# Two gate pieces in every step of part 1, and those of a split's step moved between its scores and its transposes

## The chip, the cores and the metric

The kernel runs on one core of one Trainium2 chip. A time is device microseconds (us) of one execution of the whole program. The engines are TensorE (PE; its weight loads are listed apart as PEld), VectorE (DVE), ScalarE (ACT), GpSimd (POOL) and SyncE (SP), which here only issues DMAs. Each works through its own queue of instructions in order, and they wait for each other by semaphores.

## The reference

A gated linear attention with a state per head, and a feed-forward block that multiplies two projections:

```python
# q, k, v, alpha: batch 4, heads 8, 768 positions, head size 48
for t in range(S):
    state = alpha[:, :, t, :, None] * state + einsum('bhd,bhe->bhde', k[:, :, t], v[:, :, t])
    y[:, :, t] = einsum('bhd,bhde->bhe', q[:, :, t], state)
x = y as (3072 tokens, 384)
out = ((x @ w1) * (x @ w2) @ w3) @ w_out      # d_ff 1024
```

The weights arrive as 64-bit floats.

## The kernel before

**Chunks and steps.** The 3072 positions are cut into 24 chunks of 128 (six per batch entry), and part 1 is a loop of 25 steps `n`, one chunk each. On TensorE a step holds, in this order: the state products of chunk n-1 (`attend_state`, L473 or L483), the scores of chunk n (`scores`, L431 with the lower halves of chunk n-1's attention, L420), the transposes of decayed q and k of chunk n+1 (`transposed`, L383, copied out of PSUM by ScalarE at L385), the attention of chunk n-1 (`attend`, L496; ScalarE copies y out at L493 and L498), the outer products of k and v of chunk n (`outer`, L395, taken over by VectorE at L405; none for the last chunk of a batch entry), and the sums of logarithms for chunk n+3 (`decays`, L348). VectorE masks the scores (L441, four instructions per step) and multiplies q and k by the decays (`decayed`, L361). ScalarE takes the logarithms of alpha (L326), rounds them (L330; VectorE makes the rest, L331) and makes the exponentials (L351, L352) out of the sums.

**Groups, splits, pieces.** Part 1 has room on TensorE for the first products of the feed-forward block. `EARLY` names five groups of finished chunks: four of three chunks (384 tokens) and one of four. A group begins with its split (`split_early`): x is cut into a rounded part (ScalarE, L536) and two rests (VectorE, L537 and L539), in one buffer for all groups, so a split has to wait until the products of the group before it are done. Then its gates follow: a gate is one tile of 128 of the 1024 columns, and makes x @ w1 and x @ w2 for it. Each of these two is one piece: nine matmuls of 384 columns (L569), six into one PSUM bank, which ScalarE empties (L578), and three into another, which VectorE adds (L580). After the second piece VectorE multiplies both (L617), and the product of the gate before is stored by a DMA (`store_ab`, L643, on SP's queue). The gates are generators that yield between their pieces; they lie in the queue `fill`, and `run(k)` issues the next k pieces. A group of four gates thus has eight pieces. The last group has sixteen, of which eight are left to part 2.

**Where the order comes from.** Group 0 is split in step 6, groups 1 to 4 in steps 9, 13, 17 and 21 (the steps with `n - 2 in begin`). Behind the transposes of that step the split is issued, and its gates are put into `fill`. `pieces` says how many a step issues: `run(pieces > 0)` behind the outer products, `run(pieces > 1)` behind the logarithms, `run(pieces > 2)` at the end of the step. In step 7 another `run(2)` stands behind the transposes. The framework turns this program into one queue per engine, chooses the eight PSUM banks, and may change the order of neighbours on ScalarE and VectorE; `after_marks` keeps instructions behind a named one on the same engine. Besides, `convert` works off the conversion of w1 and w2 from 64 bits a step at a time (L246 to L267, on ScalarE and VectorE).

**Part 2** makes the remaining gates, folds w3 and w_out together and makes the output. The change doesn't touch it.

Of the kernel before, what the change touches and what calls it, by code (L numbers as in the profile page):

```python
# [48 lines left out]
def kernel(  # L49
# [18 lines left out]
    N = B * NCH  # L68
# [37 lines left out]
    def bank():  # L106
        return ps.tile([C, 512], FP32, tag="bank", name="bank")
# [3 lines left out]
    def after_marks(*names):  # L111
        stack = ExitStack()
        for x in names:
            stack.enter_context(tc.issue_after(mark[x]))
        return stack
# [22 lines left out]
    def load_a(n):  # L138
        if paired(n):
            if n % 2 == 0:  # L140
                b, c = divmod(n, NCH)
                x = pairs[n // 2 % 2]
                nc.sync.dma_start(out=x.rearrange("p h s d -> p h (s d)"), in_=alpha[b, :, ds(c * C, 2 * C), :].rearrange("h (p s) d -> p h (s d)", s=2))
                st["a", n] = st["a", n + 1] = x
        elif n < N:
            st["a", n] = inp.tile([C, H, D], FP32, tag="ac", name="ac", bufs=2)
            nc.sync.dma_start(out=st["a", n], in_=rows(alpha, n))

    def load_kq(n):
        if n >= N:  # L150
            return
        st["kq", n] = inp.tile([C, 2, H, D], FP32, tag="kq", name="kq")
        nc.sync.dma_start(out=st["kq", n][:, 0], in_=rows(k, n))
        nc.sync.dma_start(out=st["kq", n][:, 1], in_=rows(q, n))

    def load_v(n):
        if n < N:
            st["v", n] = vs[n % len(vs)]
            (nc.gpsimd if 2 < n < 8 else nc.sync).dma_start(out=st["v", n][:, :, 0:D], in_=rows(v, n))
# [122 lines left out]
    def fetch(ahead=3):  # L282
        while weights and len(begun) < ahead:
            begun.append(weights.popleft())
            next(begun[-1])
# [17 lines left out]
    def store():  # L303

        while later:
            dst, src = later.popleft()
            nc.sync.dma_start(out=dst, in_=src)
# [64 lines left out]
    def transposed(n):  # L372
        if n >= N:
            return
        qk = qks[n % 3]
        qkT = work.tile([C, 2, NP, C], FP32, tag="qkT", name="qkT")

        tp = [bank().rearrange("p (i j c) -> p i j c", i=2, j=NP) for _ in range(2)]
        for i in range(2):
            for j in range(NP):  # L380
                for half in range(2):
                    s = ds(DP * half, DP)
                    nc.tensor.transpose(tp[half][:, i, j, :], qk[s, i, 2 * j:2 * j + 2, :], ident[s, s])  # L383
        for half in range(2):
            mark["qkT", n] = nc.scalar.copy(qkT[:, :, :, ds(DP * half, DP)], tp[half]).ins  # L385
        st["qkT", n] = qkT
# [30 lines left out]
    def attend_low(n, j, i):  # L417

        s, w = ds(DP * i, DP), (vts[n % 2][:, j, :] if i else st["v", n][:, 2 * j, :])
        nc.tensor.matmul(st["y", n][1][ds(DP * (1 - i), DP), j, :], w[s], st["ms", n][s, i, j, 0:DP],  # L420
                         start=(n % NCH == 0 and j == 0), stop=(j == NP - 1), skip_group_check=True)
# [94 lines left out]
    def load_early(e):  # L516

        first, chunks = EARLY[e]
        if chunks == 3:
            pieces = ((xb[0][:, XB - KM * TG:].bitcast(FP32), 3),)  # L520
        else:
            pieces = ((inp.tile([C, 2, H, D], FP32, tag="kq", name="kq").rearrange("p i h d -> p (i h d)"), 2),
                      *((inp.tile([C, H, D], FP32, tag="ac", name="ac", bufs=2).rearrange("p h d -> p (h d)"), 1) for _ in range(2)))
        st["xT", e], at = [], 0
        for x, width in pieces:
            x = x.rearrange("p (k t) -> p k t", k=KM)
            nc.sync.dma_start(out=x, in_=x_of(first + at, width))
            st["xT", e].append((x, ds(at * C, width * C)))
            at += width
# [174 lines left out]
    fill = deque()  # L704

    def run(pieces):

        for _ in range(pieces):
            if not fill:
                return  # L710
            try:
                next(fill[0])
            except StopIteration:
                fill.popleft()
# [22 lines left out]
    FIRST = 6  # L737
    begin = {FIRST - 3 + 4 * g: (g, range(FH if g < 4 else KF)) for g in range(5)}
    loads = {8: 1, 11: 2, 15: 3, 20: 4}

    def early_pair(n):
        return n in ends and n < FIRST

    for n in range(N + 1):
        if n >= FIRST:
            load_v(n + 2)
        if not 1 < n < FIRST:
            store()
        if n in loads:
            load_early(loads[n])  # L750
        if n != 1 and not 2 < n <= FIRST:
            load_a(n + 5)
        raws = (3, 3, 3, 3, 2, 2, 3, 3)[n] if n < 8 else 4
        for m in (n + 3,) * (n <= FIRST) + (n + 4,) * (n >= FIRST):
            load_kq(m)
            if 2 < n <= FIRST and m == n + 3:
                load_a(n + 5)
            if 1 < n < FIRST:
                store()
            if n < FIRST - 2:  # L760
                fetch(raws)
        late_state = early_pair(n - 1)
        if n and not late_state:
            attend_state(n - 1)
        if n < N:
            scores(n)
            if late_state:
                attend_state(n - 1)
        else:
            for j in range(NP):  # L770
                for i in range(2):
                    attend_low(n - 1, j, i)
        transposed(n + 1)
        if n == 1:
            decays(3)
            load_a(6)
            with after_marks(("e", 3)):
                logs(4)
        if n == FIRST + 1:
            run(2)  # L780
        if n - 2 in begin and n > FIRST:
            g, tiles = begin[n - 2]
            with after_marks(("ms", n), ("qkT", n + 1)):
                split_early(g)
            fill.extend(gate(g, f) for f in tiles)
        if n == FIRST:
            with after_marks("l", ("qkT", n + 1)):
                split_early(0)
            fill.extend(gate(0, f) for f in begin[n - 3][1])
        pieces = ((3, 3, 2, 0) if n > FIRST + 3 else (0, 3, 3, 0))[(n - FIRST) % 4] if n >= FIRST else 0  # L790
        if n == 0:
            with after_marks(("qkT", 0)):
                logs(2)
            decays(2)
            with after_marks(("e", 2)):
                logs(3)
        early, ready = n < FIRST, len(thirds) if n > 2 else n // 2
        marks = (*[("qkT", n + 1)] * (n < N - 1), *[("qk", n + 1), ("ms", n)] * early, *["x3"] * (n - 2 in begin and n > FIRST))
        if n < N - 2 and n != FIRST:
            with after_marks(*marks):  # L800
                convert(2 if early else 1, raws)
        with after_marks(*[("vt", n)] * turned(n)):
            advance(n)
        if n < FIRST:
            with after_marks("pool"):
                load_v(n + 2)
        if n:
            attend(n - 1)
        outer(n)
        if n > FIRST:  # L810
            third(ready)
        run(pieces > 0)
        if early:
            with after_marks(*marks):
                convert(1, raws)
        with after_marks(*[("ms", n)] * (n <= FIRST)):
            decayed(n + 2)
        if not early:
            with after_marks(*[("qkT", n + 1)] * (n < N - 4), *["scale"] * (n > FIRST)):
                logs(n + 4)  # L820
        if n == 4:
            load_early(0)
        convert(early and n > 0, raws)
        run(pieces > 1)
        if n:
            decays(n + 3)
        if n <= FIRST:
            third(ready)
        if 0 < n < FIRST:
            with after_marks(("e", n + 3)):  # L830
                logs(n + 4)
        if n == FIRST:
            with after_marks("x3", ("e", n + 3)):
                convert(2, raws)
        elif n < N - 2:
            convert(n == FIRST - 1 if early else n % 3 == 0, raws)
        if n == FIRST - 1:
            assert len(done) == 2 * KM
        turn_v(n + 1)
        run(pieces > 2)  # L840
        if n == N - 3:
            while begun:
                convert(1)
            weights.extend(load_out(j) for j in range(KF))
            fetch(4)
# [92 lines left out]
```

## Time and profile before

| | us |
|---|---|
| three runs | 456.66, 458.87, 460.57 (median 458.87) |
| the profiled execution | 456.97 |
| its span, first to last instruction | 455.2 |
| TensorE busy (4304 matmuls) | 442.2, 97% |
| its weight loads busy (4304) | 392.9, 86% |
| VectorE busy | 369.8, 81% |
| ScalarE busy | 279.3, 61% |
| GpSimd busy | 85.5, 19% |

The granted TensorE clock of the profiled execution is 0.999. A row of the profile names the kernel's line, the engine, the operation, the tile written and the tiles read, the shape, how often, the busy time and the mean in ns of one, and then the idle time just before with what ended it. Matmuls are pipelined and overlap in such rows, so lengths are better read from one start to the next. L569 is the line of a helper that issues all large matmuls; in part 1 it stands for the gates' pieces.

The steps of the stretch in question, by the start of their first matmul on TensorE (us from the span's start):

| step | 7 | 8 | 9 | 10 | 11 | 12 | 13 | 14 | 15 | 16 | 17 | 18 | 19 | 20 | 21 | 22 | 23 |
|---|---|---|---|---|---|---|---|---|---|---|---|---|---|---|---|---|---|
| start | 51.92 | 64.05 | 72.87 | 76.69 | 87.08 | 95.12 | 102.06 | 105.42 | 114.75 | 123.25 | 130.19 | 133.56 | 143.00 | 151.49 | 158.45 | 161.72 | 172.24 |
| length | 12.13 | 8.82 | 3.82 | 10.39 | 8.04 | 6.94 | 3.36 | 9.33 | 8.50 | 6.94 | 3.37 | 9.44 | 8.49 | 6.96 | 3.27 | 10.52 | 8.54 |
| pieces | 5 | 3 | 0 | 3 | 3 | 2 | 0 | 3 | 3 | 2 | 0 | 3 | 3 | 2 | 0 | 3 | 3 |

Steps 7, 13 and 19 have no state products, steps 11, 17 and 23 no outer products, steps 21 and later no logarithms.

### The profile page before, as it was taken

Reading aid. Unit: us, or ns where it says so; the run is one execution under the profiler, and the core shown is the slowest. Engines: PE = TensorE matmul, PEld = TensorE weight load, DVE = VectorE, ACT = ScalarE, POOL = GpSimd, SP = SyncE. Lnnn points to the kernel's source line nnn. Section 1 sums busy time; section 2 is a strip of 40 time slices with the busy share of each in tenths; the row PEclk is TensorE's granted clock in tenths of the full one; section 3 lists DMA queues with packets and bytes.
Section 4 is the critical chain, followed back from the end, with each engine's and each line's share of the span. In section 5 each row is a group of like instructions: output and inputs, shape, how many; then the busy total and the mean of one; then the engine's idle time right before and its main releaser. Section 6 shows DMA issues by size and latency. Waiting matters only on the chain.

```text
span 455.2 us, 11107 instructions
## 1 busy us (share of the span) xinstructions
PE 442.2 (97%) x4304; PEld 392.9 (86%) x4304; DVE 369.8 (81%) x600; ACT 279.3 (61%) x523; POOL 85.5 (19%) x171
## 2 busy tenths in 40 slices
PE   4999998999999999999999999999999999999996
PEld 2677797998988988888888888888888999999996
DVE  2799997999979898899998999999427576776671
ACT  4698966779688673978875766575436333333430
POOL 6244341335225330021121010100010000000000
PEclk9999999999999999999999999999999999999999
DMA  9999999999888763466775263600129555565411
GB/s 205 246 263 235 256 248 232 229 228 236 211 185 208 198 176 106 148 184 176 251 231 184 95 187 114 208 32 38 48 89 279 175 176 165 168 192 171 151 51 52
DMA packets 149381, 79.98 MB, mean 176 GB/s; under 512 B 97184, under 2 KB 138784, under 8 KB 149328
## 3 DMA queue, kind: packets, MB, share of 16 engines
q1 hardware_dynamic: 143840, 64.84, 53.4%
q0 software_dynamic: 5488, 14.43, 10.1%
q8 instruction: 34, 0.56, 0.5%
q14 instruction: 19, 0.16, 0.1%
HBM read 57.19 MB, written 22.06 MB: 174 GB/s over the span
## 4 chain that ended last, share of the span: by engine, by line
PE 94%; ACT 2%; DVE 1%; issue 1%; DMA 1%; DVEq 0%; ACTq 0%
PE bank L569 74%; PE bank L383 3%; PE bank L342 2%; PE bank L431 2%; PE bank L455 2%; PE bank L473 2%; PE bank L502 2%; PE bank L395 2%; PE bank L496 1%; PE bank L348 1%; PE bank L345 1%; PE bank L420 1%; PE bank L483 1%; DMA ac<-in_alpha_dram 1%; ACT x L536 0%
## 5 line engine op out<-in xcount | busy, mean ns | idle before, releaser
L569 PE MATMUL bank<-x,w 128*128 128x512 f32 (+1 forms) x688 | 161.8, 373 | 0.7 <-ACT e L352 0.4
L569 PEld LDWEIGHTS bank<-x,w 128*128 128x128 f32 x688 | 124.7, 188 | 19.6 <-ACT e L352 0.7
L569 PE MATMUL bank<-w3o,ab 128*128 128x384 f32 x576 | 100.2, 335 | 0.0
L569 PEld LDWEIGHTS bank<-w3o,ab 128*128 128x128 f32 x576 | 99.9, 188 | 0.2
L569 PE MATMUL bank<-x3b,w 128*128 128x512 f32 (+1 forms) x248 | 71.6, 384 | 0.0
L594 ACT ACTIVATE bank<-bank 128x512 f32<-128x512 f32 (+1 forms) x72 | 41.1, 571 | 32.2 <-PE bank L569 32.2
L569 PEld LDWEIGHTS bank<-x3b,w 128*128 128x128 f32 x248 | 46.5, 188 | 8.2 <-issue 0.3
L643 POOL DMA_DIRECT2D abd<-r x33 | 19.3, 583 | 140.0 <-DVE r L629 117.4
L693 DVE TENSOR_TENSOR ab<-abl,ab 128x1024 fp32r<-128x1024 f32 x24 | 29.4, 1226 | 14.3 <-ACT ab L692 14.3
L385 ACT COPY qkT<-bank 128x512 f32<-128x512 f32 x48 | 25.9, 590 | 23.8 <-PE bank L383 23.8
L578 ACT ACTIVATE t<-bank 128x384 f32<-128x384 f32 x24 | 11.8, 493 | 46.0 <-PE bank L569 46.0
L692 ACT ACTIVATE ab<-abl 128x1024 fp32r<-128x1024 f32 x24 | 25.5, 1061 | 21.7 <-PE bank L569 19.8
L569 PE MATMUL bank<-wo,w3T 128*128 128x384 f32 x192 | 36.3, 337 | 0.0
L569 PEld LDWEIGHTS bank<-wo,w3T 128*128 128x128 f32 x192 | 34.1, 188 | 1.2
L580 DVE SCALAR_TENSOR_TENSOR o<-bank,t 128x384 f32<-128x384 f32 x24 | 13.4, 558 | 25.9 <-issue 14.3
L251 ACT ACTIVATE power<-power,rebias 128x512 uint32<-128x512 uint32 (+1 forms) x36 | 25.0, 695 | 13.1 <-DVE power L250 12.9
L629 DVE TENSOR_TENSOR r<-bank,r 128x512 f32<-128x512 f32 x32 | 21.8, 682 | 9.3 <-PE bank L569 8.6
L361 DVE TENSOR_TENSOR qk<-kq,e 128x768 f32<-128x768 f32 x24 | 23.0, 957 | 7.7 <-ACT e L352 7.7
L694 DVE SCALAR_TENSOR_TENSOR ab<-ab,abl 128x1024 fp32r<-128x1024 f32 x24 | 29.2, 1218 | 0.0
L580 DVE SCALAR_TENSOR_TENSOR r<-bank,r 128x384 f32<-128x384 f32 (+1 forms) x40 | 22.9, 578 | 6.5 <-ACT r L578 5.1
L253 DVE SCALAR_TENSOR_TENSOR mant<-mant,raw 128x512 f32<-128x512 uint32 (+1 forms) x36 | 23.5, 653 | 3.2 <-ACT raw L246 3.2
L578 ACT ACTIVATE r<-bank 128x384 f32<-128x384 f32 (+1 forms) x40 | 20.5, 515 | 8.6 <-PE bank L569 7.0
(119 smaller groups left out, 748.8 us busy)
## 6 DMA issues: line engine op xcount, KB each, us to landing
abl<-abd SPq DMA_DIRECT2D x24, 512.0 KB, 4.2
abd<-r POOLq DMA_DIRECT2D x33, 256.0 KB, 3.1
raw<-in_moe_w_dram SPq DMA_DIRECT2D x64, 128.0 KB, 3.9
raw<-in_moe_w_dram SPq DMA_DIRECT2D x12, 512.0 KB, 5.3
kq<-in_k_dram SPq DMA_DIRECT2D x24, 192.0 KB, 4.8
kq<-in_q_dram SPq DMA_DIRECT2D x24, 192.0 KB, 4.6
xd<-x SPq DMA_DIRECT2D x48, 96.0 KB, 3.4
xT<-xd POOLq DMA_DIRECT2D x6, 768.0 KB, 5.3
```

What stands on the lines that cost most here:

```text
L251: nc.scalar.activation(power, power, AF.Relu, scale=2.0 ** 23, bias=rebias)
L253: nc.vector.scalar_tensor_tensor(mant, top, 2.0 ** -20, rest, op0=ALU.mult, op1=ALU.add)
L361: mark["qk", n] = nc.vector.tensor_mul(qks[n % 3][:, :, :, 0:D], st.pop(("kq", n)), st.pop(("e", n)).rearrange("p i (h d) -> p i h d", h=H ...
L385: mark["qkT", n] = nc.scalar.copy(qkT[:, :, :, ds(DP * half, DP)], tp[half]).ins
L569: nc.tensor.matmul(p, w[part][i], x[part][i], start=start and part == parts[0] and i == 0, stop=stop and part == parts[-1] and i == n - 1, ...
L578: mark["scale"] = nc.scalar.activation(t, p1, AF.Copy, scale=(1.0 + 1.0 / P) * scale).ins
L580: nc.vector.scalar_tensor_tensor(to, p2, scale, t, op0=ALU.mult, op1=ALU.add)
L594: mark["scale"] = nc.scalar.activation(p, p, AF.Copy, scale=1.0 + 1.0 / P).ins
L629: nc.vector.tensor_mul(r[0], p, r[0])
L692: nc.scalar.activation(t[:, 0], ab, AF.Copy, scale=1.0 - 2.0 ** -13)
L693: nc.vector.tensor_sub(t[:, 1], ab, t[:, 0].bitcast(FP32))
L694: nc.vector.scalar_tensor_tensor(t[:, 2], t[:, 0].bitcast(FP32), -1.0 - 1.0 / P, ab, op0=ALU.mult, op1=ALU.add)
```

## The change

The number of pieces per step is computed ahead of the transposes. In steps 7 to 9 it is 1, 3 and 2 (step 7 keeps its `run(2)` besides); in steps 10 to 21 it is 2; in the last three steps it stays 3, 3, 2. In the steps of the splits (9, 13, 17, 21) the two pieces, the last of their group, are issued ahead of the transposes, that is, behind the scores, and the split follows behind the transposes as before.

```diff
             for j in range(NP):
                 for i in range(2):
                     attend_low(n - 1, j, i)
+        pieces = (1, 3, 2)[n - FIRST - 1] if FIRST < n < FIRST + 4 else 0 if n <= FIRST else 2 if n < N - 2 else (3, 3, 2)[n - N + 2]
+        next_group = n - 2 in begin and n > FIRST
+        if next_group:
+            run(pieces)
+            assert not fill
+            pieces = 0
         transposed(n + 1)
...
                 split_early(0)
             fill.extend(gate(0, f) for f in begin[n - 3][1])
-        pieces = ((3, 3, 2, 0) if n > FIRST + 3 else (0, 3, 3, 0))[(n - FIRST) % 4] if n >= FIRST else 0
         if n == 0:
             with after_marks(("qkT", 0)):
                 logs(2)
```

| step | 7 | 8 | 9 | 10 | 11 | 12 | 13 | 14-16 | 17 | 18-20 | 21 | 22 | 23 | 24 |
|---|---|---|---|---|---|---|---|---|---|---|---|---|---|---|
| pieces before | 5 | 3 | 0 | 3 | 3 | 2 | 0 | 3, 3, 2 | 0 | 3, 3, 2 | 0 | 3 | 3 | 2 |
| pieces now | 3 | 3 | 2 | 2 | 2 | 2 | 2 | 2 each | 2 | 2 each | 2 | 3 | 3 | 2 |

## The prediction

> **What bounds the kernel now.** I read the chain that ended last first, then the busy time by stretch, then what TensorE waited for, then the order of the instructions in the stretch that the change touches. The chain in order of time says where a change can count at all:
>
> ```profile
> 103.23 0.69 PE bank L383 x16
> 103.92 0.67 ACT qkT L385 x2
> ...
> 104.86 1.18 ACT x L536
> ...
> 108.80 0.51 ACT e L352
> 109.36 3.55 PE bank L569 x18
> ...
> 182.55 269.15 PE bank L569 x1362
> ```
>
> (start, length, engine, line, count.) From 182.55 us on the chain is TensorE alone, 269 us without a break; that is part 2, and the change leaves its work as it is. So only the steps 7 to 21 of part 1, about 52 to 165 us, can give or lose. There the chain is TensorE too, except behind a split: the splits begin at step 9, 13, 17 and 21, and behind each the chain goes over to ScalarE, from the copies of the transposes (L385) through the split's rounding (L536) to the exponentials (L352), which free the PSUM bank of the next gate.
>
> The stretches from the first scores after one split to those after the next (steps 10-13, 14-17, 18-21; us, then busy us and counts):
>
> ```profile
> 76.69:105.42 28.73, 27.11 (x546) 25.20 (x545) 27.72 (x55) 22.53 (x51) 9.35 (x18) 1.00 1.00 235
> 105.42:133.56 28.14, 27.78 (x578) 25.67 (x577) 25.41 (x50) 21.42 (x50) 8.40 (x17) 1.00 0.90 205
> 133.56:161.72 28.16, 27.77 (x560) 25.32 (x559) 26.07 (x50) 20.53 (x48) 10.80 (x20) 1.00 0.80 193
> ```
>
> The columns are TensorE, its weight loads, VectorE, ScalarE, GpSimd, granted clock, DMA share, GB/s. The clock is full. VectorE is the second engine by far: 27.72 of 28.73 us in the first stretch. Whoever shortens that stretch for TensorE runs into VectorE after 1.0 us.
>
> What TensorE waited for from 57 to 183 us:
>
> ```profile
> PE bank L420 <- issue: 1.6, 1, 1.6
> PE bank L569 <- ACT e L352: 0.4, 2, 0.2
> ```
>
> One wait of 1.62 us in step 10 (77.85 to 79.46) on nothing that the profile shows, in the middle of the scores; and short ones ahead of the first gate behind a split. A busy TensorE is not TensorE at its peak, so I take step lengths instead. A full step with three pieces lasts 8.50 us where nothing is late (step 15, 114.75 to 123.25), with two pieces 6.94 (steps 12 and 16), so a piece is 1.56. By this step 10 is 1.89 too long (10.39), step 14 0.83 (9.33), step 18 0.94 (9.44), step 19 0.51 (8.49, less 0.52 for its missing state products), step 22 1.43 (10.52, against step 23's 8.54 plus 0.55 for the outer products that step 23 lacks). **In all 5.6 us are there to be won**, 1.2% of the run.
>
> **The change part by part.** It adds and removes no instruction on the compute engines and no DMA: 32 pieces before the last group, as before. It moves them: step 7 has three pieces instead of five, step 9 two instead of none; then 2,2,2,2 instead of 3,3,2,0 in steps 10-13, 14-17 and 18-21; 3,3,2 at the end stay. So the sum of TensorE's own time is the same, and only waits count.
>
> *Behind the split (steps 14, 18, 22): nothing is won.* In the split's step the pieces now stand ahead of the transposes, and the split, which overwrites the pieces' operand, behind them. From the end of the transposes to the first new gate TensorE has the same work as now: attention 0.51, outer products 0.55, decays 0.55, states 0.52, scores 1.04, transposes 0.65, attention 0.51, outer products 0.55, together 4.88 us (starts in step 13 and 15). ScalarE has the same queue too: copies, split, conversion, three copies of y, logarithm, rounding, exponentials: 103.90 to 109.30, 5.40 us without a gap. TensorE has arrived after 4.88 and gets its bank at 5.56 (103.80 to 109.36). The two moved pieces lie in front of this race and not in it, so the 0.7 us stay, and those of steps 18 and 22 likewise (step 22: VectorE's split of four chunks ends 166.91 whatever stands ahead). What goes is the 0.26 us that step 14's scores wait for masks: I cost it as 0.2 won.
>
> *Step 9 and 10: about 0.8 us won.* Pieces moved from step 7 to step 9 let the transposes of step 9 end at about 75.2 instead of 75.1 us; VectorE, busy for 12.10 of step 7's 12.13 us, has its decayed q and k for chunk 9 at 61.1, before they are asked for. Behind them ScalarE's queue is the present one (L385 at 75.18 to L352's end at 80.63, 5.45 us) plus one eviction (L578, 0.38) that the new order puts between the copies and the split: the first gate of step 10 can go at 75.2+0.1+5.45+0.38=81.1, against 81.85 now. This takes the 1.62 us wait as gone. That wait falls at the end of some 3.8 us of small matmuls with no gate in between (72.87 to 77.6); with the pieces in between the instructions come half as fast. DMA is full there, and in 77.0 to 78.3 us a single 16 KB packet of the instruction queue moves (the page: 34 packets, 0.56 MB, for 8608 loads and matmuls). So I read it as TensorE short of instructions. [...]
>
> *Steps 10 to 13: 1.4 us lost.* A step now lasts 6.94 us for TensorE, while VectorE has 27.7/4=6.9 us of work in it, in order. By the starts in its timeline an eviction (L580), a product (L617) or a rest of the logarithms (L331) takes 0.47, a decayed q and k (L361) 0.87, four masks (L441) 1.55, a conversion step 0.34 or 0.60.
>
> ```profile
> 85.44 0.95 DVE L361 TENSOR_TENSOR qk<-kq,e 128x768 f32<-128x768 f32 x1
> ...
> 97.20 0.74 DVE L441 TENSOR_TENSOR ms<-bank,keep 64x256 int32<-64x256 int32 x2
> 97.97 0.86 DVE L441 TENSOR_TENSOR ms<-bank,keep_turned 64x256 int32<-64x256 int32 x2
> ```
>
> Behind the split of step 9 (from 77.75) the same queue brings L361 for chunk 12 at 86.6, but TensorE, a piece earlier, wants its transposes at 86.3: 0.36 lost in step 11. Then L331, L580, L264, L617, masks, L267, L361, four integer steps, two L580, L617, L331, L361 bring it to the masks of chunk 12 at 95.9 to 97.45. The banks that these masks free go to the first piece's second half (wanted at 95.95, free at 96.65) and to the second piece (free at 97.45): 0.75+0.25 lost in step 12. Today a third piece per step covers just this queue. With the 0.8 won the stretch ends 0.6 later.
>
> *Steps 14 to 17: nothing.* VectorE has 2.7 us to spare; the same count finds one wait of 0.15, against the 0.2 won.
>
> *Steps 18 to 21: 1.0 lost.* In steps 18 and 19 VectorE is busy 17.3 of 17.9 us now. With a piece less in each, masks of chunk 19 come at 145.3 to 147.5 among conversions while the second piece wants its bank at 145.6: 1.1 lost where 0.5 are lost now. In step 20 the masks are 0.5 late, where now they are in time.
>
> *DMAs.* Stores of gated products on SP's queue stand in step 13, 17 and 21 one later and wait for a product that is a step old; loads of k and q behind them are two steps ahead of their use (14 us, against 4.8 to landing). POOL keeps its order but for one small load. Cost nothing; without that cover a late load would cost its 4.8.
>
> *Sum:* 0.6+0+1.0=**+1.6 us** on the profiled execution's 456.97 (span 455.2), so 458.6. From below, all covers hold and VectorE runs without a gap: -1.0 in the first stretch and nothing else. From above, each wait found is double: +4. The runs shown span 456.66 to 460.57 with the median at 458.87, 1.9 above the profiled one. A scatter of 4 us on a steady clock suggests that waits like step 10's come and go, and they should be fewer after the change; so I take half of the distance: **459.5 us**.
>
> **Rivals.** (1) *Even steps take the stalls away*, faster: the split would be ready when TensorE is. For it: the 5.6 us exist, and ScalarE is busy only 22.5 of 28.7 us. Against it: the race of 4.88 against 5.40 us behind the transposes is the same. Time: 458.87-5.6=453.3. Chance 0.12.
> (2) *VectorE becomes the bound*, slower: masks stand behind evictions and conversions, and the second bank of a gate waits for them in every two-piece step as in step 12, 1.0 us each. It decides where VectorE's work in a step passes 6.94 us; for it: 50.2 of 53.5 us busy from 51.9 to 105.4 us; against it: 4.51 us in step 16. At seven such steps besides those counted, less the 1 us won: 458.87+6=465. Chance 0.20.
> [...]
> (4) The change does not do what it says: the built order shows the pieces where the words put them, so no chance.
>
> **How the numbers follow.** The forecast (-1.0 to +4 us, no change by what can be told) has 0.68, the rivals 0.12 and 0.20. About 1%, 4.6 us, is what a measurement here tells from no change. The forecast's own range is 456.9 to 462.9; to reach part of both rivals I give 455 to 464.5.
>
> **What would show it.** Right: step 10's 1.62 us gap gone, gates of step 10 at about 81.1; still 0.6 to 0.9 us between transposes and gates over TensorE's own work in steps 14, 18, 22; new waits of the second bank on L441 in steps 12, 19 and 20; part 2 unchanged at 269 us and starting at 184. Wrong: part 2 starting before 180 (rival 1), or VectorE over 98% in all three stretches and part 2 starting after 187 (rival 2), or part 2 itself longer.

## The result and the profile after

The changed kernel takes 462.24 us (median of 10 runs, 460.76 to 466.69) against 456.94 us (10 runs, 455.31 to 460.57) for the kernel before on the same chip: 1.0119 times as long, 95% interval 1.0088 to 1.0149, or 5.3 us more. Forecast were 459.5 us, no change by what can be told, with a difference of 1.6 us by the traces. The time lies in the range, but the sign is settled, 5.3 us is more than the 4.6 us that the forecast named as telling no change from one, and the sum was three times too small. Disturbed runs are left out of every comparison here, and since the profiled executions of late_even and behind were among them, these two are not read.

The profiled execution of the changed kernel is the longest of its ten runs (466.69 us, span 465.0), so it overstates the usual loss. The end of its chain that ended last, with the stretch of steps 9 and 10 (start, length, engine, line, count):

```profile
76.45 0.65 PE bank L383 x16
77.10 0.62 PE bank L496 x16
77.71 0.48 PE bank L395 x16
78.19 0.33 SPq L159
78.61 3.55 DMA xd<-x
82.21 1.16 ACT x L536
...
84.74 1.11 PE bank L383 x14
...
192.30 269.15 PE bank L569 x1362
```

Part 2 is the same 269.15 us, and it starts at 192.30 instead of 182.55. The split's rounding (L536) starts at 82.21, 5.8 us after the transposes of step 9 begin; in the same step of the kernel before it was 1.7 (74.43 to 76.13). The chain names a DMA there; the semaphore that came last for ScalarE's queue is shown further down. The three stretches of steps 10-13, 14-17 and 18-21, in the columns of the prediction (TensorE, weight loads, VectorE, ScalarE, GpSimd, granted clock, DMA share, GB/s):

```profile
78.64:112.81 34.17, 30.51 (x546) 27.68 (x545) 29.35 (x59) 23.88 (x52) 8.82 (x18) 0.90 0.93 224
112.81:142.01 29.20, 28.70 (x578) 25.70 (x577) 25.27 (x48) 21.75 (x50) 9.74 (x20) 1.00 0.95 212
142.01:171.47 29.46, 28.00 (x560) 25.15 (x559) 25.35 (x48) 20.51 (x48) 11.53 (x18) 1.00 0.74 179
```

They were 28.73, 28.14 and 28.16. The two later ones are 1.06 and 1.30 longer, the first 5.44, at a mean granted clock of 0.90. Together that is 7.80 of the 9.75 us by which part 2 starts later; the other 1.95 us lie ahead of step 10, which starts at 78.64 instead of 76.69. What TensorE waited for between 57 and 190 us, and then ScalarE (total, times, longest):

```profile
PE bank L431 <- ACT r L578: 3.0, 1, 3.0
PE bank L569 <- DVE ms L441: 0.9, 1, 0.9
PE bank L383 <- ACT x L493: 0.5, 1, 0.5
PE bank L431 <- issue: 0.4, 1, 0.4
PE bank L569 <- ACT e L352: 0.2, 1, 0.2
```

```profile
ACT r L578 <- PE bank L569: 18.2, 17, 2.7
ACT qkT L385 <- PE bank L383: 9.1, 10, 2.2
ACT r L578 <- DMA abd<-r: 3.6, 1, 3.6
```

The 1.62 us without a cause in step 10 is gone, as forecast. In its place TensorE waits 3.03 us for an eviction, and that eviction waits 3.62 us for a DMA: the landing of the store of a gated product. No such wait was among those of the kernel before. The instructions themselves, by their timeline (start, length; in brackets the idle time before and what ended it):

```profile
71.96 2.99 SPq L154 DMA_DIRECT2D kq<-in_q_dram  x1
75.00 2.04 SPq L238 DMA_DIRECT2D raw<-in_moe_w_dram  x1
77.13 0.85 SPq L643 DMA_DIRECT2D abd<-r  x2
81.83 0.49 ACT L578 ACTIVATE r<-bank 128x384 f32<-128x384 f32 x1 [3.62 <-DMA abd<-r]
82.21 1.16 ACT L536 ACTIVATE x<-x3b 128x1152 fp32r<-128x1152 f32 x1
82.37 0.43 PE L431 MATMUL bank<-qkT 48*64 48x128 f32 x8 [3.03 <-ACT r L578]
```

A gate writes into two of the four buffers of its pool, and its product stays in one of them until its store (L643) has landed. A store is issued when the next gate is complete, and in its place on SP's queue. The pieces that moved into step 9 bring a gate there. The stores of the group's first two gates belong to step 8 now and stand on SP's queue behind all loads of that step. SP works the queue off late: they go out at 77.13, in step 9, and the wait ends 4.7 us later; in the kernel before the first of them went out at 63.47. Until then the second piece has no buffer. Its eviction L578 holds up ScalarE, with the split behind it, and keeps the bank that the scores of step 10 need.

Then the clock falls. Two stretches of the same profile, from 82.90 us and from 89.73:

```profile
82.90:89.73 6.83, 6.34 (x88) 5.83 (x79) 6.80 (x13) 6.41 (x15) 2.21 (x3) 0.50 0.96 224
89.73:92.29 2.56, 2.56 (x15) 2.31 (x14) 2.52 (x6) 1.92 (x4) 0.00 (x0) 1.00 1.10 236
```

TensorE was idle from 79.33 to 82.37, 3.04 us, and from 82.90 on the granted clock is 0.50 for 6.83 us. Other profiles of this case slow down so after shorter waits (last section).

### The profile page after: what moved, and what is told of

The parts are those of the page before. It is cut to its first block, busy times and chain, and to the rows that moved or that the text cites. A ratio compares the mean times of both kernels' runs of the same rounds, so it can differ in the third digit from the quotient of the medians.

```text
span 465.0 us, 11119 instructions
## 1 busy us (share of the span) xinstructions
PE 446.8 (96%) x4304; PEld 394.5 (85%) x4304; DVE 369.4 (79%) x600; ACT 280.1 (60%) x523; POOL 86.6 (19%) x171
## 4 chain that ended last, share of the span: by engine, by line
PE 86%; DVE 5%; DMA 3%; ACT 3%; issue 1%; SPq 1%; DVEq 0%; ACTq 0%
PE bank L569 72%; PE bank L383 3%; PE bank L431 2%; DMA xd<-x 2%; PE bank L496 2%; PE bank L473 1%; PE bank L395 1%; PE bank L342 1%; PE bank L348 1%; DVE ms L458 1%; ACT x L536 1%; PE bank L420 1%; DMA x3b<-xd 1%; PE bank L345 1%; PE bank L455 1%
## 5 line engine op out<-in xcount | busy, mean ns | idle before, releaser
L569 PE MATMUL bank<-x,w 128*128 128x512 f32 (+1 forms) x688 | 163.7, 376 | 2.0 <-DVE ms L441 0.9
L643 POOL DMA_DIRECT2D abd<-r x33 | 19.3, 584 | 139.6 <-DVE r L629 113.2
L578 ACT ACTIVATE t<-bank 128x384 f32<-128x384 f32 x24 | 11.8, 492 | 45.8 <-PE bank L569 45.8
L578 ACT ACTIVATE r<-bank 128x384 f32<-128x384 f32 (+1 forms) x40 | 20.4, 514 | 23.6 <-PE bank L569 18.2
```

What stands on the lines that cost most here:

```text
L569: nc.tensor.matmul(p, w[part][i], x[part][i], start=start and part == parts[0] and i == 0, stop=stop and part == parts[-1] and i == n - 1, ...
L578: mark["scale"] = nc.scalar.activation(t, p1, AF.Copy, scale=(1.0 + 1.0 / P) * scale).ins
```

## The experiments

Theory A: the store of step 9, with the wait, the late split and the clock that falls, is the loss. Theory B: even steps cost it in themselves, because with 6.94 us to a step VectorE's queue (masks, splits, evictions) is late. Theory C, added when the traffic came into question: the DMA engines, full until 120 us (mean share 0.99 from 0 to 100 us of the kernel before, 1.03 from there to 120, 0.74 from there to 130), set the pace. A fourth question was the forecast's race behind the split. The runs, each against the kernel before on its chip (the stretches are those of one profiled execution each, in us):

| kernel | median, before | ratio (95%) | 10-13, 14-17, 18-21 |
|---|---|---|---|
| before | 456.94 | | 28.73, 28.14, 28.16 |
| changed | 462.24, 456.94 | 1.0119 (1.0088 to 1.0149) | 34.17, 29.20, 29.46 |
| first_only | 463.12, 458.14 | 1.0093 (1.0059 to 1.0127) | 33.14, 28.17, 28.13 |
| first_pool | 459.84, 458.02 | 1.0041 (1.0009 to 1.0074) | 28.89, 28.14, 27.92 |
| late_even | 461.67, 458.14 | 1.0073 (1.0039 to 1.0107) | not read |
| late_even_b | 460.45, 458.02 | 1.0076 (1.0038 to 1.0114) | 29.55, 28.93, 29.32 |
| even_nomul | 459.39, 457.43 | 1.0038 (1.0004 to 1.0073) | 29.23, 28.60, 28.51 |
| after_pool | 463.42, 458.14 | 1.0102 (1.0064 to 1.0140) | 29.78, 28.59, 29.33 |
| after_r5 | 464.37, 458.14 | 1.0122 (1.0067 to 1.0178) | 30.56, 30.34, 29.90 |
| before_light | 458.53, 458.02 | 1.0037 (0.9998 to 1.0075) | 28.41, 28.14, 28.13 |
| after_light | 463.53, 458.02 | 1.0120 (1.0074 to 1.0166) | 31.34, 28.88, 29.49 |
| one_behind | 458.92, 458.63 | 1.0020 (0.9995 to 1.0045) | 28.87, 29.62, 28.46 |
| behind | 466.15, 458.63 | 1.0134 (1.0057 to 1.0211) | not read |
| late_behind | 462.90, 458.63 | 1.0104 (1.0064 to 1.0144) | 29.42, 30.19, 28.53 |

**One half of the change at a time.** first_only has the new steps 7 to 9 and the old steps 10 to 21:

```diff
-        pieces = (1, 3, 2)[n - FIRST - 1] if FIRST < n < FIRST + 4 else 0 if n <= FIRST else 2 if n < N - 2 else (3, 3, 2)[n - N + 2]
+        pieces = (1, 3, 2)[n - FIRST - 1] if FIRST < n < FIRST + 4 else 0 if n <= FIRST else (3, 3, 2, 0)[(n - FIRST) % 4]
```

> Edit: steps 7 to 9 run three, three and two pieces as in the changed kernel, and in the split's steps the pieces stand behind the scores; steps 10 to 21 run three, three, two and none as in the kernel before. Theory A (what costs the time is one wait in step 9: both buffers of a gated product stay taken until a store lands that stands on SP's queue behind all loads of that step, the eviction on ScalarE waits 3.6 us for it and the split waits behind the eviction): the wait of L578 for the landing of the product's store (abd<-r) is there with 2 to 4 us, the split's L536 starts at about 82 us, step 10 lasts 11 to 13.7 us, and the time is 460 to 462.5, ratio to the kernel before 1.008 to 1.012. Theory B (even steps cost it, since masks and splits are late in steps 11 to 21): these steps are the old ones, so 456 to 458, ratio 0.998 to 1.003.

Theory A's numbers came, at 1.0093. The first stretch of its profile, and the first of its waits of ScalarE from 70 to 85 us:

```profile
76.17:109.31 33.14, 30.05 (x546) 27.82 (x545) 28.76 (x57) 23.59 (x52) 9.15 (x18) 0.90 0.96 234
109.31:137.48 28.17, 27.82 (x577) 25.61 (x577) 25.46 (x50) 21.39 (x50) 8.48 (x17) 1.00 0.88 197
```

```profile
ACT r L578 <- DMA abd<-r: 3.6, 1, 3.6
```

The wait and the fallen clock are there again, and the loss ends with that stretch: 33.14 against 28.73, then 28.17 against 28.14. Nine of its ten runs have a mean clock of 0.989 to 0.993.

late_even is the other half: the old steps 7 to 9, then two pieces each.

```diff
-        pieces = (1, 3, 2)[n - FIRST - 1] if FIRST < n < FIRST + 4 else ...
+        pieces = (3, 3, 0)[n - FIRST - 1] if FIRST < n < FIRST + 4 else ...
```

> Edit: steps 7 and 8 hold the five and three pieces of the kernel before and step 9 none; steps 10 to 21 run two pieces each as in the changed kernel. Theory A (the store of step 9): no eviction stands ahead of the split in step 9, so the L578 wait for the store's landing is gone, step 10 lasts 10.4 us at most, and the time is that of the kernel before plus the small waits on masks in steps 12, 15, 19 and 20 (about 1.5 us by their lines): 457.5 to 459, ratio 1.001 to 1.005. Theory B (even steps): 461 to 462.5, ratio 1.009 to 1.012.

> Edit: late_even once more (steps 7 to 9 as before, two pieces in each of steps 10 to 21), since its profiled execution was a disturbed one and shows no waits. Ratio again 1.004 to 1.011. If even steps cost what the forecast found, only more of it, the stretches 10-13, 14-17 and 18-21 are 0.5 to 1.5 us longer than the 28.7, 28.1 and 28.2 before, with TensorE waiting for the masks (L441) in steps 12, 15, 19 and 20 and no wait of ScalarE for a store above 1 us. If a store costs here too, ScalarE waits over 2 us for the landing of abd<-r in some step.

1.0073, and 1.0076 in the second set of runs: more than theory A allows and less than theory B said. So both halves lose time. The stretches of late_even_b:

```profile
76.17:105.72 29.55, 28.46 (x545) 25.02 (x544) 28.58 (x57) 22.92 (x51) 8.48 (x18) 1.00 0.93 216
105.72:134.65 28.93, 28.45 (x578) 25.72 (x577) 25.52 (x49) 21.79 (x50) 8.75 (x18) 1.00 0.90 216
134.65:163.97 29.32, 27.82 (x560) 25.15 (x559) 25.20 (x48) 20.67 (x48) 10.13 (x20) 1.00 0.86 210
```

0.82, 0.79 and 1.16 longer than before, together 2.8, at full clock, with no wait of ScalarE for a store above 1.2 us. What TensorE waited for from 50 to 192 us is scattered:

```profile
PE bank L431 <- issue: 1.0, 1, 1.0
PE bank L569 <- DVE ms L441: 0.7, 2, 0.3
PE bank L569 <- ACT e L352: 0.4, 2, 0.2
```

The masks (L441) are in it; so is one wait of 1.03 us at 137.24, in step 18, for nothing that the profile shows.

**Is it VectorE's queue?** even_nomul is late_even with less work on VectorE:

```diff
-        nc.vector.tensor_mul(r[0], *r)
+        nc.vector.tensor_mul(*(x[:, 0:16] for x in (r[0], *r)))
```

> Edit: late_even (steps 7 to 9 as before, two pieces in each later step) with the product of a gate's two halves (L617 on VectorE) made for 16 of its 384 columns alone; the rest of the gated products is left as the first half. TensorE, SP and GpSimd have the order of late_even; VectorE and ScalarE exchange a few neighbours. It takes about 0.4 us of 6.9 from VectorE in every step and nothing from TensorE. If the 3 us of even steps are VectorE's queue (masks and splits that come late where a step gives TensorE only 6.94 us): the waits of TensorE on L441 go, the stretches fall from 29.55, 28.93, 29.32 by 0.4 to 0.9 each, ratio to the kernel before 1.001 to 1.005. If they come from ScalarE behind the split, or from stores and buffers: the stretches stay within 0.3, ratio 1.006 to 1.009.

1.0038, within the ratio that was expected if it is VectorE's queue. Its stretches:

```profile
76.52:105.75 29.23, 27.34 (x545) 25.18 (x544) 27.19 (x57) 22.75 (x51) 8.91 (x18) 1.00 0.93 213
105.75:134.35 28.60, 28.27 (x577) 25.94 (x576) 23.70 (x48) 21.66 (x50) 7.71 (x17) 1.00 0.89 211
134.35:162.86 28.51, 28.04 (x559) 25.37 (x559) 23.66 (x48) 20.45 (x48) 10.93 (x20) 1.00 0.89 216
```

VectorE has 1.4 to 1.8 us less to do in each, and they are 0.32, 0.33 and 0.81 shorter; 0.4 to 0.9 were expected, so two fall a little short. In sum 1.46 of the 2.77 us that even steps cost are gone, and the waits of TensorE on the masks are gone from the list. ScalarE's longest wait for a store is 1.1 us here and 1.2 in late_even_b, so that is not what changed. Each of the two profiles and that of the kernel before holds one wait for nothing that the profile shows (1.89, 1.03 and 1.62 us). Without these the three stretches sum to 84.45, 86.77 and 83.41 us, and 2.3 of 3.4 us would be VectorE's queue; but such a wait need not be worth its length, as before_light shows below. By the times it is half of the loss (1.0038 for 1.0076), and these two intervals overlap. Among the runs with a clock of 0.998 or more the median is 4.1 us above the kernel before in late_even_b (460.27, 456.21) and 1.4 in even_nomul (458.07, 456.68). So VectorE's queue is a part of the loss, half to two thirds by these estimates; its share is not settled. VectorE is not full in the two later stretches (25.52 of 28.93 us), so there the order of its work, and not the sum, must be what makes it late; in the first it is nearly full (28.58 of 29.55).

**Taking the store's wait away.** first_pool is first_only with all stores of gated products on GpSimd's queue:

```diff
-            (nc.gpsimd if late else nc.sync).dma_start(out=abd[:, f, ...], in_=ab)
+            nc.gpsimd.dma_start(out=abd[:, f, ...], in_=ab)
```

> Edit: the order of first_only (steps 7 to 9 three, three and two pieces, later steps as before), and all stores of gated products issued by GpSimd instead of SP. Theory A (in first_only the 5 us are the store that stands late on SP's queue, and the clock that falls after the idle time): the L578 wait of step 9 for the store falls from 3.6 below 1 us, the split's L536 starts at 76.5 to 78, the granted clock is 1.00, the stretch of steps 10 to 13 falls from 33.1 to 28.5 to 30 us, and the time to that of the kernel before, 456 to 459.5 where that is 458 (ratio 0.997 to 1.004). Theory B (moving pieces from step 7 to step 9 costs in itself): ratio 1.007 or more, with the loss spread over steps 7 to 9.

From 1.0093 to 1.0041, just over the 1.004 that theory A allowed. By its timeline the two stores leave at 68.55 and 72.24 us (in first_only both from 73.75 on), the split starts behind the copies, and the gates of step 10 come without the idle time:

```profile
72.24 0.56 POOL L643 DMA_DIRECT2D abd<-r  x1 [3.11 <-DVE r L617]
74.49 0.49 ACT L578 ACTIVATE r<-bank 128x384 f32<-128x384 f32 x1 [1.07 <-PE bank L569]
76.62 1.18 ACT L536 ACTIVATE x<-x3b 128x1152 fp32r<-128x1152 f32 x1
81.19 1.33 PE L569 MATMUL bank<-x,w 128*128 128x384 f32 x6 [0.21 <-ACT e L352]
```

```profile
77.17:106.06 28.89, 27.73 (x546) 25.12 (x545) 27.93 (x55) 22.46 (x51) 14.25 (x24) 1.00 0.99 232
```

28.89 us for 33.14, at full clock. Here theory A is shown for the profile: the place of the store on SP's queue makes the wait, the late split and the low clock. About 1.9 us stay (1.0041); the profiled execution, the shortest of its ten runs, does not show where. The clock isn't the reason for all of it. Three of the ten runs are at 0.993, but the other seven, at 0.998 or more, have a median of 458.79 us, where the fifteen such runs of the kernel before on this chip have 456.21. One wait of ScalarE for a store is left in the profile, 1.88 us in step 21.

after_pool is the same edit of the changed kernel, after_r5 a fifth buffer for the products of groups 0 to 3:

```diff
-            r.append(gw.tile([C, width], FP32, tag="g", name="r"))
+            r.append(work.tile([C, width], FP32, tag="re", name="r", bufs=5) if g < 4 else gw.tile([C, width], FP32, tag="g", name="r"))
```

> Edit: the changed kernel with all stores of gated products issued by GpSimd, on whose queue no loads of step 9 stand ahead of them. Theory A (the place of the store on SP's queue): the store is issued within 1 us of its product, the L578 wait of step 9 falls below 1.5 us, 457 to 459.5, ratio 1.000 to 1.006; a store that waits for its product now holds GpSimd's other work, which may cost up to 2 us elsewhere. Theory B (even steps): 460.5 to 463, ratio 1.008 to 1.013.

> Edit: the changed kernel with a fifth buffer for the gated products of groups 0 to 3, taken from another pool; nothing else is moved. Theory A (a buffer that the late store holds): the eviction in step 9 finds the fifth buffer free, its 3.6 us wait falls below 1, the split's L536 starts at about 77 to 78.5 us, gates of step 10 come at about 81 to 82.5, and the time is 457 to 459, ratio 1.000 to 1.005, with the granted clock back at 1.00 in every run. Theory B (even steps): the wait may go, but its place is taken by the masks, 460.5 to 462.5, ratio 1.008 to 1.012.

In both profiles the 3.6 us wait is gone (after_r5 keeps one of 1.1 us), the first stretch falls from 34.17 to 29.78 and 30.56, and the gates of step 10 start 4.0 us after the step (81.30 and 81.77). But the times do not follow: 1.0102 and 1.0122 against 1.0119. Theory A fails here as the cause of the median. The runs of the changed kernel say why: five of the ten have a clock of 1.00, and still they take 460.76 to 462.53, 3.8 to 5.6 above the median before. The three longest (463.46, 463.88 and 466.69) are those at 0.993, the clock of the profile with the wait; the usual run loses its time without the fallen clock. Whether a shorter wait for the store stands in those runs is not known, since only the longest was profiled. Even steps by themselves (1.0073 to 1.0076) and the moved pieces of steps 7 to 9 without the store's wait (1.0041) sum to 1.0114 to 1.0117, close to the changed kernel's 1.0119. Each of these is known to 0.003 or 0.004, so the sum fits and does not prove the split.

after_r5 has a cost of its own in its profile: SP's queue runs with little pause (0.05 to 0.11 us between issues from 84.23 to 87.83), a load of the decays is issued at 87.38, and ScalarE waits for it.

```profile
87.38 0.40 SPq L147 DMA_DIRECT2D ac<-in_alpha_dram  x1
93.19 0.53 ACT L326 ACTIVATE la<-ac 128x384 f32<-128x384 f32 x1 [2.22 <-DMA ac<-in_alpha_dram]
```

**Is it the traffic?** The two light kernels load no v from chunk 9 on:

```diff
-            (nc.gpsimd if 2 < n < 8 else nc.sync).dma_start(out=st["v", n][:, :, 0:D], in_=rows(v, n))
+            if n < 9:
+                (nc.gpsimd if 2 < n < 8 else nc.sync).dma_start(out=st["v", n][:, :, 0:D], in_=rows(v, n))
```

> Edit: the kernel before without the loads of v from chunk 9 on; those steps compute with the v of an earlier chunk. It leaves out 15 loads of 192 KB, 2.9 MB, about 12 us of what the 16 DMA engines move at 235 GB/s. Theory C (the DMA engines, full until 120 us, set part of part 1's pace): faster than the kernel before by 1.5 to 4 us, and with less scatter. If DMA is only cover: ratio 0.998 to 1.002.

> Edit: the changed kernel without the same 15 loads of v. They stand on SP's queue ahead of the stores of gated products, one per step. Theory A and C (the store of step 9 waits behind that step's loads on full DMA engines): the store goes out and lands earlier, the 3.6 us wait of L578 falls below 2, and the time is 456 to 459, so that at least 2 of the 5 us between the changed kernel and the kernel before are gone when both are light. Theory B (even steps, by masks and splits): the changed kernel stays 4 to 6 us above the light kernel before.

1.0037 and 1.0120: nothing is won in either, and the distance between them stays 5 us. Theory C falls as far as 2.9 MB can tell. In the light changed kernel ScalarE waits 4.49 us for the store, which SP issues from 72.97 on, 2.4 us after the start of step 9 where it is 5.6 in the changed kernel, and which has landed only at 78.46. Without the loads of v the store leaves earlier, and the wait is no shorter. The light kernel before is of use in another way: its profile has no wait of 0.5 us or more in step 10, and still step 10 lasts 9.80 us with three pieces where 8.50 is a full step, against 10.39 with the 1.62 us wait. Without that wait TensorE is early and waits for ScalarE instead (0.21 us for the exponentials): the 1.62 us were worth 0.6 in the step and 0.3 in the stretch (28.41 for 28.73).

**The race behind the split.** one_behind is the kernel before with one piece of each group behind the transposes of the split's step:

```diff
+        if n - 2 in begin and n > FIRST + 3:
+            run(1)
...
-        pieces = ((3, 3, 2, 0) if n > FIRST + 3 else (0, 3, 3, 0))[(n - FIRST) % 4] if n >= FIRST else 0
+        pieces = ((3, 3, 2 - (n < N), 0) if n > FIRST + 3 else (0, 3, 3, 0))[(n - FIRST) % 4] if n >= FIRST else 0
```

> Edit: the kernel before with the last piece of each group (steps 12, 16, 20) moved into the split's step (13, 17, 21), behind the transposes and ahead of the split: three, three, one and one. It tests the race behind the split: TensorE's way from the transposes to the next gate grows by a piece, 4.88 + 1.56 = 6.44 us; ScalarE's queue starts its split when that piece has read its operand, about 0.9 us later than now, 5.4 + 0.9 = 6.3 us. If the race is what the 0.7 us gaps in steps 14 and 18 come from, they close to under 0.2 and the time falls by 1 to 2 us, ratio 0.996 to 0.998. If the gate waits for something else, or the later split only delays everything behind it: the gaps stay, ratio 1.000 to 1.004.

1.0020, no change. The race was turned round, and nothing was won. In step 14 of its profile:

```profile
107.36 1.66 DVE L537 TENSOR_TENSOR x<-x3b,x 128x1152 fp32r<-128x1152 f32 x1
109.56 1.34 PE L569 MATMUL bank<-x,w 128*128 128x384 f32 x6
110.75 0.74 DVE L441 TENSOR_TENSOR ms<-bank,keep 64x256 int32<-64x256 int32 x2
111.51 0.87 DVE L441 TENSOR_TENSOR ms<-bank,keep_turned 64x256 int32<-64x256 int32 x2
111.63 0.58 PE L569 MATMUL bank<-x,w 128*128 128x384 f32 x2 [0.73 <-DVE ms L441]
```

The gate starts at 109.56 without waiting for the exponentials (L352), for which it waited 0.21 at 109.36 before. But VectorE's half of the split (L537) starts at 107.36 instead of 106.29, the masks come behind it, and the gate's second bank waits 0.73 us for them. Step 14 lasts 10.11 us instead of 9.33.

behind and late_behind put both pieces of a split's step behind the transposes, in the changed kernel and in late_even:

```diff
+        transposed(n + 1)
         if next_group:
             run(pieces)
             assert not fill
             pieces = 0
-        transposed(n + 1)
```

> Edit: the changed kernel with the two pieces of a split's step behind the next chunk's transposes instead of in front of them (steps 9, 13, 17, 21); nothing else. Race: TensorE 4.88 + 3.12 = 8.0 us, ScalarE 5.4 + 2.45 = 7.85: gaps of 0.7 in steps 14 and 18 close, 1 to 2 us less than the changed kernel, ratio to the kernel before 1.006 to 1.010. The masks of the other steps stay late, so not under 1.004. If the later split costs more than the gaps: 1.012 to 1.018. The store of step 9 and its wait may move by a microsecond either way.

> Edit: late_even (steps 7 to 9 as before, then two pieces each) with the two pieces of steps 13, 17 and 21 behind the transposes. late_even stood at 1.0073 and 1.0076. By the race its gaps in steps 14 and 18 close, 1 to 2 us less: 1.003 to 1.006; what is left over the kernel before is then the masks alone. If the place of the pieces makes no difference: 1.006 to 1.009.

1.0134 and 1.0104, against 1.0119 and 1.0073 to 1.0076 with the pieces in front: nothing is won by it, as far as four runs of each can tell. In late_behind's profile step 14 is 8.14 us long where late_even_b's has 7.62, and the list of TensorE's waits is headed by VectorE:

```profile
PE bank L569 <- DVE tmp L405: 2.8, 2, 1.8
```

The longer of these two waits stands ahead of the first gate of step 22:

```profile
170.22 2.93 PE L569 MATMUL bank<-x,w 128*128 128x512 f32 x6 [1.80 <-DVE tmp L405]
172.94 1.15 PE L569 MATMUL bank<-x3b,w 128*128 128x512 f32 x3
...
176.01 1.52 PE L569 MATMUL bank<-x,w 128*128 128x512 f32 x6
177.37 0.84 PE L569 MATMUL bank<-x3b,w 128*128 128x512 f32 x3
```

Behind the wait six matmuls take 2.72 us to the next start, where six of the same shape take 1.36 later in the step: half the rate. From the start of step 22 to part 2 this profile takes 23.39 us, where late_even_b's takes 20.79. By the medians the placement in front of the transposes, which the change uses, is the better of the two; the intervals overlap. No kernel here beats the one before.

## Why the prediction was right or wrong

It was right inside its range and wrong in its sum: +1.6 us by the traces, +5.3 measured. Part 2 starts at 192.30 us in the profile, where 184 was to be the sign of being right. That the range holds the time is luck in part: 5.3 us are more than the forecast's own upper bound of +4, and the base they were added to was taken 1.9 us too high. As far as the runs tell, the median's 5.3 us are some 3.4 of even steps, where 2.4 were forecast, and 1.9 of the pieces moved among steps 7 to 9, where 0.8 were to be won. By its own steps:

- *Behind the split nothing is won:* right. The first gate of step 14 waits the same 0.21 us for L352 (116.75 us), and the step is 0.67 us longer than a full one with two pieces. The reason given was too simple: ScalarE's 5.40 us are one of two queues that end nearly together. one_behind took ScalarE out of the race, and VectorE's masks took its place.
- *Step 9 and 10, 0.8 us won:* the wait of 1.62 us is gone as said, and where no store is in the way the gate comes 4.0 us after the step's start (4.4 by the forecast, 5.16 before). It is worth 0.3 in the stretch (28.41 in before_light for 28.73). The small matmuls ahead of the wait lasted 4.7 us by the stated times (72.87 to 77.6), not 3.8. In the changed kernel itself the gate comes at 87.66 instead of the forecast's 81.1.
- *Steps 10 to 13, 1.4 lost:* of the right size. Against the first stretch of before_light, which has no wait like the 1.62 us (and loads no v), late_even_b loses 1.14 and after_pool 1.37. The shares were off: in late_even_b step 11 lasts 7.12 us and step 12 7.53, which is 0.73 and 0.59 too long (by 6.94 - 0.55 = 6.39 and 6.94), where 0.36 and 1.00 were forecast.
- *Steps 14 to 17, nothing:* wrong by 0.5 to 1.1 us (after_pool 28.59, late_even_b 28.93, the changed kernel 29.20 for 28.14). No single wait makes it: late_even_b's steps 15, 16 and 17 last 7.39, 7.22 and 6.70 us, 0.45, 0.28 and 0.21 too long (by 6.94, and 3.37 + 2 x 1.56 = 6.49 for the split's step). Step 15's falls to 0.13 in even_nomul, so that one was VectorE's; step 16 does not move, and its cause is open.
- *Steps 18 to 21, 1.0 lost:* right, 1.16 to 1.30. The wait of the second bank for the masks is in the changed kernel's list with 0.90 us, at 155.17, as forecast for step 19.
- *"DMAs ... Cost nothing":* **a step that failed.** I looked at whether the loads behind a store come in time, and at steps 13, 17 and 21. I did not ask what the store itself holds: a buffer that the next gate needs, in step 9, where a gate stands ahead of the split on ScalarE. It costs 3.0 us of TensorE's time and about 2 more of clock where it comes (step 10 of first_only 14.77 us, of first_pool 9.84). It makes the profiled execution and not the median: after_pool and after_r5 are without it and take as long.
- *The pieces of steps 7 to 9:* forecast without a loss of their own, and **the term that is furthest off at the median**; first_pool's 1.0041 puts it at 1.9 us (0.4 to 3.4). That number holds the moved stores too, and the kernel before with its stores on GpSimd was not run. Where the time goes is open: step 10 starts at 76.17 to 77.89 us in the profiles with the old steps 7 to 9, and at 76.17 to 79.00 in those with the new ones.
- *The base:* half of the distance from the profiled execution to the median of three runs was added. Ten runs have their median at 456.94, where the profiled execution was; the 0.9 us were not there. Nor is the scatter one "on a steady clock": of the 25 runs of the kernel before on first_pool's chip nine have a clock of 0.995 or 0.996 and a median of 459.16 us, and fifteen have 0.998 or more and 456.21. The forecast's own range from 456.9 begins 1 us lower than its -1.0 gives from the base of 458.87.

Rival 1 (stalls go, 453.3) is refuted: they return elsewhere. Rival 2 (VectorE, 465) comes nearer: even steps cost time, and VectorE's late work is a part of it. Its condition was wrong; VectorE is at 86 to 87% in the changed kernel's two later stretches, not above 98%, and the wait on the masks in every step, 1.0 us each, did not come. The forecast read step 10's wait as TensorE short of instructions. That is not shown: the wait is gone in the changed kernel, but waits of the same kind, 1.03 and 1.89 us, stand in late_even_b at step 18 and in even_nomul at step 10, and none of the runs shows what they wait for.

## What to carry over

Before moving work past a DMA issue, ask of each store which buffer it keeps taken, who needs that buffer next, and what stands behind that one on its engine: the store's delay was paid there, 3.62 us on ScalarE and 3.03 on TensorE in the changed kernel's profile. A step whose engines end nearly together gave nothing for one stall removed (one_behind, 1.0020); take the next-late queue's time as the gain's upper bound. Spreading work evenly over steps lost time here (1.0073 to 1.0076), half to two thirds of it by estimate where the uneven step was what covered a second engine's backlog.

## What the hardware showed

In the changed kernel TensorE's granted clock went to 0.50 a half microsecond (82.37 to 82.90) after a wait of 3.04 us had ended, and stayed there for 6.83 us. In first_only a wait of 2.98 us ends at 79.84; the mean clock is 0.96 in the stretch ahead of that and 0.52 in the 6.76 us behind it:

```profile
76.17:79.84 3.67, 0.69 (x33) 0.55 (x32) 0.02 (x1) 0.54 (x2) 0.88 (x3) 0.96 1.00 285
79.84:86.60 6.76, 6.65 (x101) 6.14 (x102) 6.72 (x12) 6.65 (x15) 2.21 (x3) 0.52 0.82 197
86.60:90.94 4.34, 4.34 (x26) 4.09 (x24) 4.03 (x9) 3.62 (x9) 0.00 (x0) 1.00 1.16 268
```

So a wait of 3 us cost 5 in step 10 of first_only (14.77 us, 9.84 in first_pool). The length of one wait does not tell whether the clock falls. Behind a wait of 1.80 us the matmuls of late_behind ran at half the rate (2.72 us for six, 1.36 later). after_light, with waits of 1.22 and 0.26 us among small matmuls at the start of its first stretch, has a mean clock of 0.89 in that stretch of 31.34 us, by estimate 6.9 us at one half. But 1.89 us (even_nomul) and 1.62 us (the kernel before) left the stretch's clock at 1.00. What else decides it, no run here shows, nor what brings the full clock back: in first_only TensorE was busy for 6.65 of the 6.76 us before it was at 1.00 again, in the changed kernel for 6.34 of 6.83.

A run's mean clock shows this without a profile. Half clock for 6.83 us of 465.0 gives 0.993 by estimate, which is the mean clock of the changed kernel's profiled run. 0.995 and 0.996 are 3 to 5 us by the same estimate; by this the nine runs of the kernel before at 0.995 or 0.996 had such a stretch too.
